# Chunked attention and a multiplicative FFN on one core: first loads reordered, first four units turned on TensorE, DMA turns moved later

## Chip, cores, metric

One core of a Trainium2 chip. Times are device microseconds (us) of one execution. A quoted time is the median of its runs; before and after were run at least three times each. Ratios are the mean time of one kernel's fast runs over that of the other's fast runs of the same rounds, so not quite the ratio of the medians. An interval in brackets is the 95% interval of that ratio. Where nothing else is said, the runs quoted are fast ones (no run more than 1.5% above the fastest of its kernel). The engines: PE is TensorE (PEld its weight loads), DVE VectorE, ACT ScalarE, POOL GpSimd, and SP SyncE, which here only issues DMAs. A DMA *lands* when the last of its completion signals comes in the trace.

## The reference, cut to what matters

```python
# q, k, v: [B=8, H=8, S=576, D=64] float32; chunks of 64 tokens, softmax within the chunk
scores = (q_chunk @ k_chunk.T) / sqrt(D);  attn = softmax(scores);  o = attn @ v_chunk
x = o.transpose(0, 2, 1, 3).reshape(4608, 512)          # 4608 tokens, 512 channels
out = ((x @ w1) * (x @ w2)) @ w3 @ w_out                # d_ff = 1024
```

The kernel computes in bf16 and multiplies `w3 @ w_out` once, in the prologue (`w3o`).

## The kernel before, where it matters

A *unit* is 128 tokens, two chunks: 36 units, 4.5 per sequence. An FFN tile takes 512 tokens, four units. To *turn* a tile means to transpose it in 128x128 blocks. q and k arrive token by token and must be turned before the scores; the attention result `xn` is turned into `xt` before the FFN. All turns are DMA transposes issued by SP, in program order, from SBUF to SBUF. All loads, which also cast float32 to bf16 (the page counts 38.8 MB read from HBM and 19.4 MB moved by GpSimd's queue), are issued by GpSimd. Matmuls, turns and loads each keep their program order.

```python
def load(dst, src): return inorder(nc.gpsimd.dma_start(dst, src))
def turn(dst, src): return inorder(nc.sync.dma_start_transpose(dst, src))

def turn_qk(b, i0, i1): ...        # cut: up to three turns, of q, k and the last half unit, of sequence b

def do_PV(u):
    ...                            # cut: products into PSUM, reciprocal, multiplication into xn
    turn(xt[:, :, u * UT:(u + 1) * UT], xn[:].rearrange("p n t d -> p (n t d)"))

# prologue: loads with turns between them; sequence 1 is turned before any x
load_w(wo, ...); load_w3(0); load_qk(0, 0); turn_qk(0, 0, 1); load_w3(1); load_qk(0, 1); turn_qk(0, 1, 2)
load_v(0)                          # 8 loads, one for each head
...                                # cut: rest of sequence 0, w3, w1, w2
load_batch(1); load_v(1); turn_qk(1, 0, NP + 1); load_batch(2); load_v(2)

def S_step(u):                     # scores; at a change of sequence all of the next one is turned
    do_S(u)
    b = (2 * u + 2) // NCH
    if b != (2 * u) // NCH and b + 1 < B:
        turn_qk(b + 1, 0, NP + 1)
        if b + 2 < B: load_batch(b + 2)

for u in range(UPT + 1): ...       # cut: w3 transposes, w3o and attention of units 0 to 3
# FFN tile t (16 groups of matmuls), with attention of the units of tile t+1 between its groups,
# and the output matmuls of tile t-1
```

The softmax here doesn't subtract the row's maximum and nothing guards it: scores larger than these inputs give would overflow.

## Time and profile before

| | before |
|---|---|
| median time (runs) | 325.7 us (322.4 to 326.9) |
| span of the profiled run | 323.9 us |
| first FFN matmul | 82.7 us |
| TensorE (PE) busy, whole span | 243 us, 75% |
| PE waits of over 0.5 us after the first FFN matmul | 25.5 us |

The page of the kernel before has the span in 40 slices of 8.1 us. A digit is the busy share in tenths; `PEclk` is the granted clock.

```profile
PE   0248067007899302999988996999999999999995
PEclk9987667655999855999997998999999999999999
DMA  7999999999999999999999999796593141231113
```

PE has two holes of over 19 us, in slices 8 and 9 and in slices 14 to 16. The DMA engines are busy for about 25 slices, 200 us. Stretches say the same in numbers (the columns are named in the first line):

```profile
core 0: us, PE busy (x) PEld busy (x) DVE busy (x) ACT busy (x) POOL busy (x), PEclk, DMA share, GB/s
83.00:200.00 117.00, 91.51 (x916) 42.38 (x914) 36.75 (x66) 35.42 (x62) 61.83 (x78) 0.90 1.74 157
200.00:324.00 124.00, 120.13 (x973) 55.27 (x971) 41.00 (x70) 44.44 (x78) 5.86 (x8) 0.98 0.46 92
```

So there is a *loading phase*, with the DMA moving 157 GB/s, in which PE is busy 78% of the time, and after 200 us a phase in which PE is busy 97%. PE's timeline shows the ends of the holes. In the brackets are the idle time before and what ended it:

```profile
74.67 0.44 PE L59 MATMUL xp<-vbuf_80,e 64*64 64x65 bf16 x16 [19.75 <-DVE xn L174]
...
82.67 7.07 PE L59 MATMUL a_ps<-xt,w_74 128*128 128x512 bf16 x32 [1.16 <-DMA xt<-xn]
...
127.36 1.89 PE L59 MATMUL a_ps<-xt,w_74 128*128 128x512 bf16 x4 [19.48 <-DMA xt<-xn]
```

SP's timeline has the cause. Its columns are the start and the time that SP itself was held; a line of several turns (x4) runs from the first start to the last end, waits between them included:

```profile
57.17 3.71 SPq L69 DMA_TRANSPOSE qT<-q_sb  x1
61.06 4.51 SPq L69 DMA_TRANSPOSE kT<-k_sb  x1
65.68 1.20 SPq L69 DMA_TRANSPOSE qkT<-qk_sb  x1
66.98 10.41 SPq L69 DMA_TRANSPOSE xt<-xn  x4
...
104.98 6.14 SPq L69 DMA_TRANSPOSE qT<-q_sb  x1
111.29 7.33 SPq L69 DMA_TRANSPOSE kT<-k_sb  x1
118.78 1.21 SPq L69 DMA_TRANSPOSE qkT<-qk_sb  x1
120.09 23.73 SPq L69 DMA_TRANSPOSE xt<-xn  x5
```

x of units 0 to 3 is turned from 67 us on, behind the turns of sequence 1, which wait for their data; x of unit 7 is turned at 120 us, behind those of sequence 3. The first hole ends with products (`xp`) and not with the FFN, because the multiplication into `xn` waited for one of its two buffers, which an x turn sets free: by the view of the tile xn, it waited 23.3 us for x turns.

### The profile page before, as it was taken

Reading aid. Unit: us, or ns where it says so; the run is one execution under the profiler, and the core shown is the slowest. Engines: PE = TensorE matmul, PEld = TensorE weight load, DVE = VectorE, ACT = ScalarE, POOL = GpSimd, SP = SyncE. Lnnn points to the kernel's source line nnn. Section 1 sums busy time; section 2 is a strip of 40 time slices with the busy share of each in tenths; the row PEclk is TensorE's granted clock in tenths of the full one; section 3 lists DMA queues with packets and bytes.
Section 4 is the critical chain, followed back from the end, with each engine's and each line's share of the span. In section 5 each row is a group of like instructions: output and inputs, shape, how many; then the busy total and the mean of one; then the engine's idle time right before and its main releaser. Section 6 shows DMA issues by size and latency. Waiting matters only on the chain.

```text
span 323.9 us, 5311 instructions
## 1 busy us (share of the span) xinstructions
PE 243.1 (75%) x2144; PEld 113.4 (35%) x2144; DVE 87.1 (27%) x155; ACT 88.1 (27%) x153; POOL 123.1 (38%) x163
## 2 busy tenths in 40 slices
PE   0248067007899302999988996999999999999995
PEld 0214033003344101444433442444444444444442
DVE  0001111002064100454331332334334343341310
ACT  1011012000523200343341432343343333423232
POOL 8486425967719725902940880070000000000000
PEclk9987667655999855999997998999999999999999
DMA  7999999999999999999999999796593141231113
GB/s 96 175 148 178 177 195 163 180 172 139 171 162 142 180 155 156 144 88 180 158 150 212 131 154 209 122 115 116 120 157 69 49 97 53 80 68 50 47 67 130
DMA packets 179816, 43.35 MB, mean 134 GB/s; under 512 B 171088, under 2 KB 174160, under 8 KB 179792
## 3 DMA queue, kind: packets, MB, share of 16 engines
q0 software_dynamic: 117200, 19.41, 86.6%
q1 hardware_dynamic: 57408, 14.16, 29.4%
q10 hardware_dynamic: 5184, 9.44, 9.1%
q8 instruction: 17, 0.28, 0.4%
q14 instruction: 7, 0.06, 0.1%
HBM read 38.80 MB, written 9.44 MB: 149 GB/s over the span
## 4 chain that ended last, share of the span: by engine, by line
PE 61%; DMA 27%; POOL 5%; issue 3%; SPq 2%; DVE 1%; ACT 0%; POOLq 0%; DVEq 0%
PE a_ps L59 20%; PE b_ps L59 20%; PE o_ps L59 17%; DMA xt<-xn 9%; DMA w_75<-in_moe_w_dram 6%; DMA k_sb<-in_k_dram 3%; DMA w_76<-in_moe_w_dram 3%; PE sp L59 3%; DMA q_sb<-in_q_dram 3%; DMA vbuf_80<-in_v_dram 2%; SPq L69 2%; DMA vbuf_81<-in_v_dram 2%; PE xp L59 2%; POOL vbuf_81 L65 1%; POOL vbuf_80 L65 1%
## 5 line engine op out<-in xcount | busy, mean ns | idle before, releaser
L59 PE MATMUL a_ps<-xt,w_74 128*128 128x512 bf16 x288 | 75.9, 391 | 26.1 <-DMA xt<-xn 23.2
L198 DVE TENSOR_TENSOR ab<-a_sb,b_ps 128x512 bf16<-128x512 f32 x72 | 49.5, 688 | 113.3 <-PE b_ps L59 113.3
L59 PE MATMUL b_ps<-xt,w_75 128*128 128x512 bf16 x288 | 75.8, 390 | 0.0
L59 PE MATMUL o_ps<-w3o,ab 128*128 128x512 bf16 x288 | 67.3, 379 | 0.0
L191 ACT COPY a_sb<-a_ps 128x512 f32<-128x512 f32 x72 | 42.1, 585 | 83.0 <-PE a_ps L59 76.6
L59 PEld LDWEIGHTS <-w_74 128*128 128x128 bf16 x288 | 26.5, 100 | 57.1 <-DMA xt<-xn 19.6
L59 PEld LDWEIGHTS <-w_75 128*128 128x128 bf16 x288 | 28.7, 100 | 35.5 <-issue 3.4
L59 PEld LDWEIGHTS <-ab 128*128 128x128 bf16 x288 | 27.9, 98 | 33.4
L210 ACT COPY o_sb<-o_ps 128x512 f32<-128x512 f32 x36 | 21.1, 586 | 66.6 <-PE o_ps L59 66.6
L65 POOL DMA_DIRECT2D k_sb<-in_k_dram x32 | 30.2, 943 | 7.9 <-DMA w_75<-in_moe_w_dram 2.5
L65 POOL DMA_DIRECT2D q_sb<-in_q_dram x32 | 30.3, 947 | 6.6 <-DMA w_75<-in_moe_w_dram 2.5
L174 DVE TENSOR_TENSOR xn<-xp,rc 128x512 bf16<-128x512 f32 x36 | 24.9, 692 | 24.6 <-DMA xt<-xn 23.3
L65 POOL DMA_DIRECT2D vbuf_81<-in_v_dram x24 | 17.5, 750 | 30.8 <-PE xp L59 19.0
L155 ACT ACTIVATE e<-sp 128x512 bf16<-128x512 f32 x36 | 21.6, 601 | 22.3 <-PE sp L59 21.5
L65 POOL DMA_DIRECT2D vbuf_80<-in_v_dram x24 | 17.6, 760 | 24.6 <-PE xp L59 20.2
L59 PE MATMUL sp<-qT,kT 64*64 64x64 bf16 x512 | 14.9, 197 | 12.6 <-DMA kT<-k_sb 12.6
L59 PE MATMUL wp<-wo,w3T 128*128 128x512 bf16 x64 | 22.5, 520 | 0.0
L229 ACT CAST w3o<-wp 128x512 bf16<-128x512 f32 x8 | 4.7, 585 | 60.1 <-PE wp L59 60.1
L62 PE MATMUL w3tp<-ident,w_76 128*128 128x128 bf16 x64 | 7.1, 278 | 18.0 <-DMA w_76<-in_moe_w_dram 18.0
L59 PE MATMUL xp<-vbuf_80,e 64*64 64x65 bf16 x216 | 5.7, 202 | 19.7 <-DVE xn L174 19.7
L172 DVE RECIPROCAL rc<-xp 128x8 f32<-128x8 f32 x36 | 7.4, 207 | 47.7 <-PE xp L59 47.6
L59 PEld LDWEIGHTS <-kT 64*64 64x64 bf16 x512 | 11.0, 110 | 25.6 <-DMA kT<-k_sb 13.3
(25 smaller groups left out, 76.1 us busy)
## 6 DMA issues: line engine op xcount, KB each, us to landing
out_dram<-o_sb ACTq DMA_DIRECT2D x36, 256.0 KB, 2.2
q_sb<-in_q_dram POOLq DMA_DIRECT2D x32, 128.0 KB, 8.0
k_sb<-in_k_dram POOLq DMA_DIRECT2D x32, 128.0 KB, 8.0
w_76<-in_moe_w_dram POOLq DMA_DIRECT2D x8, 256.0 KB, 8.9
vbuf_80<-in_v_dram POOLq DMA_DIRECT2D x24, 72.0 KB, 4.3
vbuf_81<-in_v_dram POOLq DMA_DIRECT2D x24, 72.0 KB, 5.0
vbuf_82<-in_v_dram POOLq DMA_DIRECT2D x16, 72.0 KB, 5.7
wo<-in_moe_w_out_dram POOLq DMA_DIRECT2D x1, 1024.0 KB, 9.5
```

What stands on the lines that cost most here:

```text
L59: return inorder(nc.tensor.matmul(*a, **kw))
L62: return inorder(nc.tensor.transpose(*a, **kw))
L65: return inorder(nc.gpsimd.dma_start(dst, src))
L69: return inorder(nc.sync.dma_start_transpose(dst, src))
L155: nc.scalar.activation(e[:], sp[:], Exp, scale=scale, bias=0.0)
L172: nc.vector.reciprocal(rc[:], xv[:, :, :, D:D + 1])
L174: nc.vector.tensor_mul(xn[:].rearrange("p n t d -> p t n d"), xv[:, :, :, 0:D], rc.to_broadcast([P, 2, NHP, D]))
L191: nc.scalar.copy(a_t[j][:], a_ps[:])
L198: nc.vector.tensor_mul(ab_t[t][:, j, :], a_t.pop(j)[:], b_ps[:])
L210: nc.scalar.copy(o_sb[:], o_ps[:])
L229: nc.scalar.copy(w3o[:, ko, :], wp[:])
```

## The change

Intent: let the FFN start earlier. The first four units no longer need the DMA for turns (PE transposes them, between the groups of `w3 @ w_out`), loads come in an order that serves this and in larger pieces, and turns of later sequences no longer stand ahead of x. The second FFN tile is halved, so that its first half needs two units only. Besides, q/k get three buffers instead of two, `xn` three as well, the heads lie in another order in the buffers, and the scores use four 64x64 quadrants of the array (`64*64` in the trace) in turn instead of two.

```diff
 def load_v(b):                                   # two loads instead of eight
-    for h in range(H): load(vbuf[...one head...], v[b, h]...)
+    for t in range(2): load(vbuf[...four heads...], v[b, t * NHP:(t + 1) * NHP]...)
-    qk_t[b] = (io.tile(q, bufs=2), io.tile(k, bufs=2), io.tile(qk, bufs=2))
+    qk_t[b] = io.tile([P, G, DM], bf, tag="qk", bufs=3)        # nine groups: q, k, q, k, ..., last
+def pe_turn_qk(b, g):
+    tp = ps.tile([P, NHP, P], bf, tag="m", bufs=4)
+    for n in range(NHP): tr(tp[:, n, :], qk_t[b][:, g, n * P:(n + 1) * P], ident[:])
+    nc.vector.tensor_copy(qkT_tile(b)[:, g], tp[:])
+def pe_turn_x(u): ...                            # the same from xn to xt
-load_w3(0); load_qk(0,0); turn_qk(0,0,1); load_w3(1); ...; load_batch(1); load_v(1); turn_qk(1, ...)
+load_w3(0,1); load_w3(1,2); load_qk(0,0); load_qk(0,1); load_w3(2,3); load_v(0); ...   # no turns here
-for u in range(UPT + 1): do_S(u); do_w3T(u + 2); do_w3o(u + 1); PV_step(u - 1)
+do_w3T(0); do_w3T(1); do_w3o(0); pe_turn_unit(0); pe_turn_unit(1); do_w3o(1); ...; pe_turn_x(3); do_w3o(7)
+tiles = [(0, 512), (512, 256), (768, 256), (1024, 512), ...]
+pieces = ((0, 4), (4, 8), (8, 9))                # turns of the next sequence, one piece each at
 def S_step(u):                                   # chunks 2, 4 and 6 of this one
-    turn_qk(b + 1, 0, NP + 1)
+    if b > 1 and c in (2, 4, 6): turn_qk(b + 1, *pieces[c // 2 - 1])
+    if b == 1 and c == 7: ...                    # all pieces of sequence 2
```

(Scores, buffers and placing of the steps are shortened.)

More of the change, by code (lines that the diff above doesn't have):

```diff
@@ L82 @@
         nc.vector.memset(vbuf[i][:, :, :, D:D + 1], 1.0)
+    NP = S // UT
+    G = 2 * NP + 1
     qk_t, qkT_t = {}, {}
-    NP = S // UT
     def rows(src, b, t0, n):
@@ L94, in load_qk @@
         if b not in qk_t:
-            qk_t[b] = (io.tile([P, NP, DM], bf, tag="q", name="q_sb"),
-                       io.tile([P, NP, DM], bf, tag="k", name="k_sb"),
-                       io.tile([P, DM], bf, tag="qk", name="qk_sb"))
+            qk_t[b] = io.tile([P, G, DM], bf, tag="qk", bufs=3, name="qk")
         if i < NP:
-            for t, src in zip(qk_t[b], (q, k)):
-                load(t[:, i, :].rearrange("p (h d) -> p h d", d=D), rows(src, b, i * UT, UT))
+            for t, src in enumerate((q, k)):
+                load(qk_t[b][:, 2 * i + t, :].rearrange("p (h d) -> p h d", d=D),
+                     rows(src, b, i * UT, UT))
@@ L101, in load_qk @@
         else:
             for p0, src in ((0, q), (CH, k)):
-                load(qk_t[b][2][p0:p0 + CH, :].rearrange("p (h d) -> p h d", d=D),
+                load(qk_t[b][p0:p0 + CH, 2 * NP, :].rearrange("p (h d) -> p h d", d=D),
                      rows(src, b, NP * UT, CH))
-    def turn_qk(b, i0, i1):
-        if b not in qkT_t:
-            qkT_t[b] = (io.tile([P, NP * NHP, P], bf, tag="qT", name="qT"),
-                        io.tile([P, NP * NHP, P], bf, tag="kT", name="kT"),
-                        io.tile([P, NHP, P], bf, tag="qkT", name="qkT"))
-        if i0 < NP:
-            i = min(i1, NP)
-            for t in range(2):
-                turn(qkT_t[b][t][:, i0 * NHP:i * NHP, :],
-                     qk_t[b][t][:, i0:i, :].rearrange("p c m -> p (c m)"))
-        if i1 > NP:
-            turn(qkT_t[b][2][:], qk_t[b][2][:])
@@ L119, in qT, with load_batch @@
-    def qT(b, c, hp):
-        if c // 2 < NP:
-            return qkT_t[b][0][:, c // 2 * NHP + hp, c % 2 * CH:(c % 2 + 1) * CH]
-        return qkT_t[b][2][:, hp, 0:CH]
-    def kT(b, c, hp):
-        if c // 2 < NP:
-            return qkT_t[b][1][:, c // 2 * NHP + hp, c % 2 * CH:(c % 2 + 1) * CH]
-        return qkT_t[b][2][:, hp, CH:P]
+    def load_batch(b):
+        for i in range(NP + 1):
+            load_qk(b, i)
     def load_v(b):
-        for h in range(H):
-            n, hh = divmod(h, 2)
-            load(vbuf[b % NV][hh * CH:(hh + 1) * CH, n, :, 0:D],
-                 v[b, h].rearrange("(c p) d -> p c d", p=CH))
+        for t in range(2):
+            load(vbuf[b % NV][t * CH:(t + 1) * CH, :, :, 0:D].rearrange("p n c d -> p (n c) d"),
+                 v[b, t * NHP:(t + 1) * NHP].rearrange("n (c p) d -> p (n c) d", p=CH))
@@ L135, in load_w, with qkT_tile, turn_qk @@
     def load_w(dst, ap, n0, n1):
         load(dst[:, :, n0:n1], ap.rearrange("(ko p) n -> p ko n", p=P)[:, :, n0:n1])
+    def qkT_tile(b):
+        if b not in qkT_t:
+            qkT_t[b] = io.tile([P, G, NHP, P], bf, tag="qkT", name="qkT")
+        return qkT_t[b]
+    def turn_qk(b, g0, g1):
+        turn(qkT_tile(b)[:, g0:g1].rearrange("p g n t -> p (g n) t"),
+             qk_t[b][:, g0:g1, :].rearrange("p g m -> p (g m)"))
+    def pe_turn_qk(b, g):
+        tp = ps.tile([P, NHP, P], bf, tag="m", bufs=4, name="qktp")
+        for n in range(NHP):
+            tr(tp[:, n, :], qk_t[b][:, g, n * P:(n + 1) * P], ident[:])
+        nc.vector.tensor_copy(qkT_tile(b)[:, g], tp[:])
@@ L139, in chunk_at, with at @@
+    def at(b, c, n, isk):
+        i, o = divmod(c, 2)
+        if i < NP:
+            return qkT_t[b][:, 2 * i + isk, n, o * CH:(o + 1) * CH]
+        return qkT_t[b][:, 2 * NP, n, isk * CH:(isk + 1) * CH]
     def chunk_at(u, ci):
         return divmod(2 * u + ci, NCH)
-    e_t = {}
+    NM = NHP // 2
+    e_t, xn_t = {}, {}
     def do_S(u):
-        sp = ps.tile([P, NHP, 2, CH], f32, tag="s", name="sp")
+        sp = ps.tile([P, 2, 512], f32, tag="s", name="sp")
+        sv = sp[:, :, 0:NHP * CH].rearrange("p r (m c q) -> p r m c q", m=NM, c=2)
@@ L146, in do_S @@
         for ci in range(2):
             b, c = chunk_at(u, ci)
-            for hp in range(NHP):
-                for hh in range(2):
-                    h = slice(hh * CH, (hh + 1) * CH)
-                    mm(sp[h, hp, ci, :],
-                       lhsT=kT(b, c, hp)[h], rhs=qT(b, c, hp)[h],
-                       start=True, stop=True)
-        e = asb.tile([P, NHP, 2, CH], bf, tag="e", name="e")
-        nc.scalar.activation(e[:], sp[:], Exp, scale=scale, bias=0.0)
+            for m in range(NM):
+                for t in range(2):
+                    for r in range(2):
+                        h = slice(r * CH, (r + 1) * CH)
+                        mm(sv[t * CH:(t + 1) * CH, r, m, ci, :],
+                           lhsT=at(b, c, 2 * t + m, 1)[h], rhs=at(b, c, 2 * t + m, 0)[h],
+                           start=True, stop=True)
@@ L156, in do_S @@
+        e = asb.tile([P, 2, NM, 2, CH], bf, tag="e", name="e")
+        nc.scalar.activation(e[:].rearrange("p r m c q -> p r (m c q)"), sp[:, :, 0:NHP * CH],
+                             Exp, scale=scale, bias=0.0)
         e_t[u] = e
@@ L161, in do_PV @@
         W = D + 1
-        for hp in range(NHP):
-            for ci in range(2):
-                b, c = chunk_at(u, ci)
-                for hh in range(2):
-                    h = slice(hh * CH, (hh + 1) * CH)
-                    mm(xp[ci * CH:(ci + 1) * CH, hh, hp * W:(hp + 1) * W],
-                       lhsT=e[h, hp, ci, :], rhs=vbuf[b % NV][h, hp, c, 0:W],
-                       start=True, stop=True)
+        for m in range(NM):
+            for r in range(2):
+                for ci in range(2):
+                    b, c = chunk_at(u, ci)
+                    for t in range(2):
+                        h = slice(t * CH, (t + 1) * CH)
+                        n = 2 * m + r
+                        mm(xp[ci * CH:(ci + 1) * CH, t, n * W:(n + 1) * W],
+                           lhsT=e[h, r, m, ci, :], rhs=vbuf[b % NV][h, n, c, 0:W],
+                           start=True, stop=True)
         xv = xp[:, :, 0:NHP * W].rearrange("p t (n w) -> p t n w", w=W)
@@ L172, in do_PV, with turn_x, pe_turn_x @@
         nc.vector.reciprocal(rc[:], xv[:, :, :, D:D + 1])
-        xn = asb.tile([P, NHP, 2, D], bf, tag="xn", name="xn")
-        nc.vector.tensor_mul(xn[:].rearrange("p n t d -> p t n d"), xv[:, :, :, 0:D],
-                             rc.to_broadcast([P, 2, NHP, D]))
-        turn(xt[:, :, u * UT:(u + 1) * UT], xn[:].rearrange("p n t d -> p (n t d)"))
+        xn = asb.tile([P, 2, NHP, D], bf, tag="xn", bufs=3, name="xn")
+        nc.vector.tensor_mul(xn[:], xv[:, :, :, 0:D], rc.to_broadcast([P, 2, NHP, D]))
+        xn_t[u] = xn[:].rearrange("p t n d -> p (t n d)")
+    def turn_x(u):
+        turn(xt[:, :, u * UT:(u + 1) * UT], xn_t.pop(u))
+    def pe_turn_x(u):
+        xn = xn_t.pop(u)
+        tp = ps.tile([P, NHP, P], bf, tag="m", bufs=4, name="xtp")
+        for n in range(NHP):
+            tr(tp[:, n, :], xn[:, n * P:(n + 1) * P], ident[:])
+        nc.vector.tensor_copy(xt[:, :, u * UT:(u + 1) * UT], tp[:])
+    tiles = [(0, TT), (TT, TT // 2), (TT + TT // 2, TT // 2)]
+    tiles += [(t0, TT) for t0 in range(2 * TT, NT, TT)]
     ab_t, a_t = {}, {}
     def mm_ab(w, dst, t, j):
-        xs = xt[:, :, t * TT:(t + 1) * TT]
+        t0, n = tiles[t]
         for ki in range(KO):
-            mm(dst[:], lhsT=w[:, ki, j * P:(j + 1) * P], rhs=xs[:, ki, :],
+            mm(dst[:, 0:n], lhsT=w[:, ki, j * P:(j + 1) * P], rhs=xt[:, ki, t0:t0 + n],
                start=(ki == 0), stop=(ki == KO - 1))
     def do_a(t, j, tag="a_sb", bufs=2):
+        n = tiles[t][1]
         a_ps = ps.tile([P, TT], f32, tag="m", bufs=4, name="a_ps")
@@ L190, in do_a @@
         a_t[j] = msb.tile([P, TT], f32, tag=tag, bufs=bufs, name="a_sb")
-        nc.scalar.copy(a_t[j][:], a_ps[:])
+        nc.scalar.copy(a_t[j][:, 0:n], a_ps[:, 0:n])
     def do_b(t, j):
+        n = tiles[t][1]
         if t not in ab_t:
@@ L197, in do_b @@
         mm_ab(w2, b_ps, t, j)
-        nc.vector.tensor_mul(ab_t[t][:, j, :], a_t.pop(j)[:], b_ps[:])
+        nc.vector.tensor_mul(ab_t[t][:, j, 0:n], a_t.pop(j)[:, 0:n], b_ps[:, 0:n])
     def do_ab(t, j):
@@ L210, in do_o @@
         nc.scalar.copy(o_sb[:], o_ps[:])
-        r0 = t * TT + n * P
+        r0 = tiles[t][0] + n * P
         inorder(nc.scalar.dma_start(out[r0:r0 + P, :], o_sb[:]))
@@ L219, in do_w3T @@
             tr(tp[:, ki, :], w3[:, ko, ki * P:(ki + 1) * P], ident[:])
-        w3T_t[ko] = msb.tile([P, FO, P], bf, tag="w3T", name="w3T")
+        w3T_t[ko] = msb.tile([P, FO, P], bf, tag="w3T", bufs=3, name="w3T")
         nc.vector.tensor_copy(w3T_t[ko][:], tp[:])
@@ L232, with load_w3 @@
     w3v = moe_w3.rearrange("(ko p) n -> p ko n", p=P)
-    def load_w3(ko):
-        load(w3[:, ko, :], w3v[:, ko, :])
-    def load_batch(b):
-        for i in range(NP + 1):
-            load_qk(b, i)
+    def load_w3(k0, k1):
+        load(w3[:, k0:k1, :], w3v[:, k0:k1, :])
     load_w(wo, moe_w_out, 0, DM)
@@ L245 @@
         fill=1.0, base=0, pattern=[[-1, P]], channel_multiplier=1))
-    load_w3(0)
+    load_w3(0, 1)
+    load_w3(1, 2)
     load_qk(0, 0)
-    turn_qk(0, 0, 1)
-    load_w3(1)
     load_qk(0, 1)
-    turn_qk(0, 1, 2)
+    load_w3(2, 3)
     load_v(0)
-    load_w3(2)
+    load_w3(3, 4)
     load_qk(0, 2)
-    turn_qk(0, 2, 3)
-    load_w3(3)
     load_qk(0, 3)
-    load_qk(0, 4)
-    turn_qk(0, 3, 5)
-    for ko in range(4, FO):
-        load_w3(ko)
+    load_w3(4, 6)
+    load_w3(6, 8)
     HF = DF // 2
@@ L265 @@
             load_w(w, ap, n0, n0 + HF)
-    load_batch(1)
+    load_qk(0, 4)
+    load_qk(1, 0)
+    load_qk(1, 1)
     load_v(1)
-    turn_qk(1, 0, NP + 1)
+    for i in range(2, NP + 1):
+        load_qk(1, i)
     load_batch(2)
     load_v(2)
+    pieces = ((0, 4), (4, 8), (8, 9))
     def S_step(u):
         do_S(u)
-        b = (2 * u + 2) // NCH
-        if b != (2 * u) // NCH and b + 1 < B:
-            turn_qk(b + 1, 0, NP + 1)
-            if b + 2 < B:
-                load_batch(b + 2)
+        for ci in range(2):
+            b, c = chunk_at(u, ci)
+            if b == 0:
+                continue
+            if c == 0 and b + 2 < B:
+                load_batch(b + 2)
+            if b + 1 < B:
+                if b > 1 and c in (2, 4, 6):
+                    turn_qk(b + 1, *pieces[c // 2 - 1])
+                if b == 1 and c == 7:
+                    for p in pieces:
+                        turn_qk(2, *p)
     def PV_step(u):
         do_PV(u)
+        turn_x(u)
         b = (2 * u + 2) // NCH
@@ L285, in PV_step, with pe_turn_unit @@
             load_v(b + 2)
+    def pe_turn_unit(i):
+        pe_turn_qk(0, 2 * i)
+        pe_turn_qk(0, 2 * i + 1)
     do_w3T(0)
@@ L289, with place @@
     do_w3o(0)
-    for u in range(UPT + 1):
-        if u < UPT:
-            do_S(u)
-        if u + 2 < FO:
-            do_w3T(u + 2)
-        do_w3o(u + 1)
-        if u > 0:
-            PV_step(u - 1)
+    pe_turn_unit(0)
+    pe_turn_unit(1)
+    do_w3o(1)
+    do_w3T(2)
+    do_S(0)
+    do_w3o(2)
+    do_S(1)
+    do_PV(0)
+    do_w3T(3)
+    do_w3o(3)
+    do_PV(1)
+    pe_turn_unit(2)
+    pe_turn_unit(3)
+    pe_turn_x(0)
+    do_w3T(4)
+    do_S(2)
+    do_w3T(5)
+    do_w3o(4)
+    pe_turn_x(1)
+    do_S(3)
+    do_PV(2)
+    do_w3T(6)
+    do_w3o(5)
+    do_PV(3)
+    pe_turn_x(2)
     do_w3T(7)
     do_w3o(6)
+    pe_turn_x(3)
     do_w3o(7)
-    fill, slots = [], {}
+    fill, units = [], {}
+    def place(d, *what):
+        units.setdefault(len(fill) + d, []).extend(what)
     for j in range(FO):
@@ L307 @@
         fill.append(lambda j=j: do_b(0, j))
-    slots[14] = (UPT, None)
-    slots[15] = (UPT + 1, UPT)
-    slots[16] = (UPT + 2, UPT + 1)
-    slots[17] = (UPT + 3, UPT + 2)
-    slots[18] = (UPT + 4, UPT + 3)
+    place(-2, lambda: (turn_qk(0, 8, 9), turn_qk(1, 0, 2), turn_qk(1, 2, 4)))
+    place(0, lambda: S_step(4), lambda: turn_qk(1, 4, 6))
+    place(1, lambda: S_step(5))
+    place(2, lambda: PV_step(4))
+    place(3, lambda: PV_step(5), lambda: turn_qk(1, 6, 8), lambda: turn_qk(1, 8, 9))
     for n in range(UPT):
         fill.append(lambda n=n: do_o(0, n))
-    for t in range(1, NTT):
-        for n in range(UPT):
-            if t + 1 < NTT:
-                u = (t + 1) * UPT + n
-                slots[len(fill)] = (u + 1, u)
+    place(0, lambda: S_step(6))
+    place(2, lambda: S_step(7))
+    place(3, lambda: PV_step(6))
+    place(5, lambda: PV_step(7))
+    for j in range(FO):
+        fill.append(lambda j=j: do_ab(1, j))
+    place(0, lambda: S_step(8))
+    us = list(range(8, NU))
+    for t in range(2, len(tiles)):
+        no = tiles[t - 1][1] // P if t > 1 else 0
+        for n in range(4):
+            if us:
+                u = us.pop(0)
+                if u + 1 < NU:
+                    place(0, lambda u=u: S_step(u + 1))
+                place(0, lambda u=u: PV_step(u))
             fill.append(lambda t=t, j=2 * n: do_ab(t, j))
             fill.append(lambda t=t, j=2 * n + 1: do_ab(t, j))
-            if t > 1:
+            if n < no:
                 fill.append(lambda t=t, n=n: do_o(t - 1, n))
     for n in range(UPT):
-        fill.append(lambda n=n: do_o(NTT - 1, n))
+        fill.append(lambda n=n: do_o(len(tiles) - 1, n))
     for i, f in enumerate(fill):
-        if i in slots:
-            us, up = slots[i]
-            if us < NU:
-                S_step(us)
-            if up is not None:
-                PV_step(up)
+        for g in units.get(i, ()):
+            g()
         f()
```

## The prediction

> **What bounds the kernel now.** From about 130 us TensorE (PE) is nearly full: the stretches 140-160 and 200-280 show it busy throughout; one 512-token FFN tile with attention takes 23.1 us. Before that it starves: the timeline has the first FFN matmul at 82.7 us, after only some 30 us of PE work. The large holes are 55-74.7 and 107.9-127.4 us. The chain of waits explains the first: loads until w2 lands (51.05), then q/k and v of sequence 1, then SP turns q/k of sequence 1, and only then x of sequence 0. In SP's timeline x of unit 0, whose xn is done at 33 us, is turned at 67, behind three turns of sequence 1. The second hole is alike: x of unit 7 queues behind q/k turns of sequence 3 (105-119).
>
> **What the change does.**
> 1. Sequence 0's first four units need no DMA turn: 32 PE transposes of q/k and 16 of x, 4-5 us of PE (a w3 group of 8 takes 0.62-1.04), 12 more copies of about 0.7 us on DVE, 27% busy. Gone: x waiting for sequence 1, and 1.5 MB of turns.
> 2. Loads: v in 2 instead of 8, w3 partly in pairs. Each load waits for the one eight before it, so larger ones keep more in flight. Loads alone land at about 157 GB/s of bf16 (128 KB each 0.84 us). The 6.9 MB up to w2 are through at about 44 us (51 before, shared with turns). Estimate.
> 3. Second FFN tile halved: its first half needs only units 4 and 5.
> 4. Turns go in pieces between the x turns.
> 5. Scores use four 64x64 quadrants instead of two; S+PV cost 0.6 us per unit (steps of 5.79 against 5.18); I expect 0.1 less each, 3 us in all.
>
> **Sum.** PE starts at 12 us (wo and first w3, unchanged) with 33 us of dense prologue work, so out of the half-speed state that follows idling (w3o groups of 8 take 3.2 us after a hole, 1.89 without[...]). First FFN matmul at about 49 us, 34 earlier. Tile 0 with outputs ends at 71. New stalls follow, because each next tile's x is computed just before its use, and a turn takes 0.9 us on DVE plus 6-7 to land under load: 6 us before the first half tile, 7 around S of unit 9 (turns of sequence 2 sit behind x of unit 7), 5 before tile 3, 3 later. Tile 3 starts at about 112; one tile of 19 us, five of 22.8, a last of 20.7, 10 of tail: 283 plus 2 outside the profiled span.
>
> DMA limits this: a 512-token tile costs it about 10 us of loads, 8 of turns (198 GB/s alone at 200-205 us), 3 of output, 21 of PE's 23. So waits on xt may grow.
>
> **Predicted: 286 us, range 276 to 301.** Faster by over 2%: 0.97; within 2%: 0.02; slower: 0.01.
>
> **Signs.** First a_ps matmul at 46-53 us; the holes at 55-75 and 108-127 gone; several 3-8 us waits of PE for xt or qkT between 70 and 115; steady tiles at 22.5-23 us; SP's first turn after 44 us.
>
> **What would make it wrong.** DMA saturating after 70 us, so that late turns stall PE in every tile (300 or more); hand-offs holding the prologue (FFN at 55+); shorter landings, which erase the stalls (275).

Four things that the prediction says of the hardware, as before shows them:

- Four w3o groups of 8 soon after holes of 1.7 to 9.0 us took 3.15 to 3.45 us; two that followed such work without a hole took 1.89. From 60 to 75 us, in a hole, the granted clock was 0.50. It was 0.54 to 0.60 in three of the slow groups, but 1.00 in the fourth (at 15.86 us), whose slowness it therefore does not show.
- The ninth load was issued at 11.07 us, after a wait of 2.86 us that the landing of the first (wo) ended. That larger loads keep more in flight was an estimate.
- Loads alone moved 154 GB/s from 54 to 57 us.
- The packets of the output queue took 9.1% of the 323.9 us span, 3.3 us for each of nine tiles.

## More of the kernel before

The experiments ran later, on three chips, where the median of before was 323.7 to 326.5 us; where a comparison with after hangs on a few us, the ratios are the safer measure.

The FFN of tile t+1 needs x of all its units. The products of its last unit run only two pairs of FFN groups (3.5 us) and one output group (1.7 us) before it starts.

How long a turn of x takes from its issue to its landing is in the view of the tile xt:

```profile
DMA to landing us min/median/max: 2.4/4.4/7.5
```

## The result

| | before | after |
|---|---|---|
| median time (runs) | 325.7 us | 313.3 us (312.1 to 313.7) |
| ratio | | 0.963 [0.957, 0.970] |
| span of the profiled run | 323.9 us | 311.3 us |
| first FFN matmul | 82.7 us | 40.0 us |
| PE waits of over 0.5 us after it | 25.5 us | 52.4 us |
| rest of the span (span less the two) | 215.7 us | 218.9 us |

The FFN starts 42.6 us sooner, and the kernel ends 12.6 us sooner by the profile. The last two rows say where the other 30 us went: 26.9 us into new waits of PE, 3.2 us into the rest. The slices of the page after (7.8 us each):

```profile
PE   0497999909319604993999229989999999999995
PEclk9999999967958955999699859997999999999999
DMA  6999999999999999999999997992275322311013
```

The prologue is now dense, and behind it are five large holes. The DMA row hardly changed. The stretches of after:

```profile
40.00:190.00 150.00, 99.70 (x997) 50.43 (x996) 39.12 (x76) 38.49 (x73) 67.97 (x78) 0.82 1.88 157
190.00:311.00 121.00, 115.40 (x958) 52.14 (x956) 39.90 (x69) 43.28 (x76) 2.30 (x2) 0.98 0.44 94
```

This is the whole result in two lines. The loading phase still runs at 157 GB/s, and it ends near 190 us, not much earlier than before: by the trace the last q/k load lands at 190.6 us (199.7 in before). PE entered it 43 us sooner, but was busy for 99.7 us of it (66%), where before it was busy for 91.5 us. PE's timeline shows the waits:

```profile
40.03 7.07 PE L59 MATMUL a_ps<-xt,w_74 128*128 128x512 bf16 x32
...
64.91 0.33 PE L59 MATMUL sp<-qkT 64*64 64x64 bf16 x8 [2.39 <-DMA qkT<-qk]
70.48 1.01 PE L59 MATMUL a_ps<-xt,w_74 128*128 128x256 bf16 x4 [5.25 <-DMA xt<-xn]
...
92.40 0.43 PE L59 MATMUL sp<-qkT 64*64 64x64 bf16 x16 [11.54 <-DMA qkT<-qk]
...
109.52 0.32 PE L59 MATMUL sp<-qkT 64*64 64x64 bf16 x8 [3.25 <-DMA qkT<-qk]
...
121.04 1.89 PE L59 MATMUL a_ps<-xt,w_74 128*128 128x512 bf16 x4 [10.98 <-DMA xt<-xn]
122.73 1.91 PE L59 MATMUL b_ps<-xt,w_75 128*128 128x512 bf16 x4
...
148.56 1.86 PE L59 MATMUL a_ps<-xt,w_74 128*128 128x512 bf16 x4 [5.89 <-issue]
...
184.53 1.86 PE L59 MATMUL a_ps<-xt,w_74 128*128 128x512 bf16 x4 [11.00 <-issue]
```

"issue" in the last two means that the view found no releaser close by; the x turns that these tiles need landed at 148.47 and 184.44 us, 0.09 us ahead of each, so they too are waits for x. After a wait the first groups ran at half speed: from 121.04 us on, two groups of four matmuls start 1.69 us apart, against 0.86 to 0.87 in a steady stretch of a tile (129 to 132 us). The granted clock was 0.50 from 121.0 to 124.4 us and 1.00 from 156 to 172 us; after the waits that ended at 70.5, 92.4 and 148.6 us it was 0.50 too (for the next 2.5 to 3.5 us), after the one at 184.5 us 0.60.

The wait at 184 is the one to study. Its x is that of unit 19, whose products are done by 168 us. SP's timeline of after:

```profile
166.22 1.64 SPq L69 DMA_TRANSPOSE xt<-xn  x1
168.06 7.56 SPq L69 DMA_TRANSPOSE qkT<-qk  x1
175.73 1.26 SPq L69 DMA_TRANSPOSE xt<-xn  x1
```

SP was held for 7.56 us by issuing a 512 KB turn of q/k, then issued the turn of x at 175.73, and that landed at 184.44, 8.7 us later: 17 us from products to use, with 5 us of matmuls to cover them. The turn of q/k itself had landed only at 182.29, 2.15 us before x, so part of these 8.7 us may be time behind it on the same queue. It can't be all of it: the x turns issued at 130.24 and 157.62, when every earlier turn had landed, still took 7.1 and 8.0 us. The view of the tile xt, after:

```profile
DMA to landing us min/median/max: 2.4/6.9/9.8
```

The minimum is as before; the median went from 4.4 to 6.9 us. Two theories suggested themselves. **Volume**: in the loading phase the DMA must move its bytes at 157 GB/s, and PE can't run ahead of them. **Landing**: the bytes suffice, but a few turns that PE needs at once take 7 to 17 us because other traffic is in their way.

### The profile page after: what moved, and what is told of

The parts are those of the page before. It is cut to its first block, busy times and chain, and to the rows that moved or that the text cites. A ratio compares the mean times of both kernels' runs of the same rounds, so it can differ in the third digit from the quotient of the medians.

```text
span 311.3 us, 5443 instructions
## 1 busy us (share of the span) xinstructions
PE 240.8 (77%) x2256; PEld 117.6 (38%) x2256; DVE 92.2 (30%) x175; ACT 89.4 (29%) x161; POOL 93.8 (30%) x113
## 4 chain that ended last, share of the span: by engine, by line
PE 68%; DMA 22%; issue 4%; DVE 3%; POOL 1%; SPq 1%; ACT 0%; DVEq 0%; POOLq 0%
PE a_ps L59 21%; PE b_ps L59 19%; PE o_ps L59 18%; DMA xt<-xn 16%; PE wp L59 5%; DMA qkT<-qk 4%; DMA w_76<-in_moe_w_dram 3%; PE sp L59 2%; PE xp L59 2%; DVE xn L181 1%; PE w3tp L62 1%; DVE w3T L241 1%; DVE qkT L130 1%; SPq L69 1%; DVE ab L218 0%
## 5 line engine op out<-in xcount | busy, mean ns | idle before, releaser
L59 PE MATMUL a_ps<-xt,w_74 128*128 128x512 bf16 (+1 forms) x320 | 80.9, 383 | 35.2 <-DMA xt<-xn 18.3
L218 DVE TENSOR_TENSOR ab<-a_sb,b_ps 128x512 bf16<-128x512 f32 (+1 forms) x80 | 50.7, 634 | 126.9 <-PE b_ps L59 126.6
L59 PE MATMUL b_ps<-xt,w_75 128*128 128x512 bf16 (+1 forms) x320 | 78.8, 375 | 0.0
L210 ACT COPY a_sb<-a_ps 128x512 f32<-128x512 f32 (+1 forms) x80 | 43.4, 543 | 90.9 <-PE a_ps L59 89.6
L59 PEld LDWEIGHTS <-w_74 128*128 128x128 bf16 x320 | 30.4, 103 | 65.6 <-issue 25.7
L65 POOL DMA_DIRECT2D qk<-in_k_dram x40 | 34.1, 853 | 42.6 <-DMA qk<-in_k_dram 17.9
L59 PEld LDWEIGHTS <-w_75 128*128 128x128 bf16 x320 | 32.7, 102 | 34.5 <-issue 5.1
L65 POOL DMA_DIRECT2D qk<-in_q_dram x40 | 34.1, 852 | 28.0 <-DMA qk<-in_q_dram 11.5
L159 ACT ACTIVATE e<-sp 128x512 bf16<-128x512 f32 x36 | 21.6, 601 | 27.0 <-PE sp L59 26.9
L59 PE MATMUL sp<-qkT 64*64 64x64 bf16 x576 | 12.2, 202 | 17.2 <-DMA qkT<-qk 17.2
L59 PEld LDWEIGHTS <-qkT 64*64 64x64 bf16 x576 | 7.9, 110 | 30.7 <-DMA qkT<-qk 17.5
L65 POOL DMA_DIRECT2D vbuf_81<-in_v_dram x6 | 6.9, 1149 | 19.0 <-PE xp L59 14.5
## 6 DMA issues: line engine op xcount, KB each, us to landing
qk<-in_q_dram POOLq DMA_DIRECT2D x32, 128.0 KB, 12.6
qk<-in_k_dram POOLq DMA_DIRECT2D x32, 128.0 KB, 12.6
```

The lines of the kernel that those rows point to most:

```text
L59: return inorder(nc.tensor.matmul(*a, **kw))
L159: nc.scalar.activation(e[:].rearrange("p r m c q -> p r (m c q)"), sp[:, :, 0:NHP * CH], Exp, scale=scale, bias=0.0)
L210: nc.scalar.copy(a_t[j][:, 0:n], a_ps[:, 0:n])
L218: nc.vector.tensor_mul(ab_t[t][:, j, 0:n], a_t.pop(j)[:, 0:n], b_ps[:, 0:n])
```

## The experiments

All are edits of the kernel after unless said otherwise. Each kernel gave four runs, beside seven or eight of before on the same chip. "Waits" are PE's idle times of over 0.5 us after its first FFN matmul, in the profiled run.

### Bytes or landings: e2, e4, e9

**e2_x_on_pe.** All x are turned on PE, one pair of FFN groups after their products.

```diff
 def PV_step(u):
-    do_PV(u); turn_x(u)
+    do_PV(u)
+    place(1, lambda u=u: pe_turn_x(u))     # one step later; likewise for units 4 to 7
```

> Every x is turned on PE (4 transposes and one DVE copy per unit) instead of by DMA, for all units and not only the first four. Both A and B expect it to gain: 3.7 MB of turns leave the DMA (23 us at 156 GB/s) and the 35 us of waits for xt go, for about 28 x 0.35 = 10 us more PE work. A: 285-292. B: 288-296, with waits for qkT growing. If instead PE or DVE hand-offs cost more than thought: over 300.

Measured: 279.7 us, ratio to before 0.864 [0.859, 0.869]. That is 34 us below after (32 by the ratios), and below both ranges expected, for a few moved lines; 32 turns left the DMA, not the 28 that the expectation counted. Waits 15.6 us. The slices and the stretch of the loading phase:

```profile
PE   0297899993987907999999999999999999999993
DMA  6999999999999999999999999999971111111223
```

```profile
40.00:190.00 150.00, 133.86 (x1421) 69.34 (x1420) 60.45 (x122) 51.62 (x97) 70.51 (x80) 0.94 1.91 160
```

The DMA is as busy as ever (160 GB/s until 190 us), yet PE is busy 89% of the phase. A busy DMA was not in itself the limit.

**e4_qk_part_on_pe.** The control: nearly as many bytes of turns taken from the DMA, but turns of q/k.

```diff
-    if b > 1 and c in (2, 4, 6): turn_qk(b + 1, *pieces[c // 2 - 1])
+    if b > 1 and c == 2:                    # and at c == 7 of sequence 1; groups 0-3 of sequence 1 too
+        for g in range(4): pe_turn_qk(b + 1, g)
+    if b > 1 and c in (4, 6): turn_qk(b + 1, *pieces[c // 2 - 1])
```

> Control for e2_x_on_pe: the same number of turns (28 of 128 KB, 3.7 MB) leaves the DMA for PE, but they are turns of q/k (the first four groups of sequences 1 to 7); all x after the first four units stays on the DMA. If e2 gained its 34 us by relieving the DMA of bytes (volume), this gains about the same: 278-288. If e2 gained because nothing waits for the landing of an x turn any more (latency), the waits for xt stay, shortened, and only the 17 us of waits for qkT go: 295-303.

Measured: 307.2 us, ratio 0.943 [0.939, 0.947]. The waits for qkT went, those for x stayed, as the view of waits has it for e4 (who waited for what: us in total, times, longest):

```profile
PE a_ps L59 <- DMA xt<-xn: 37.6, 6, 12.2
```

The trace has 38.1 MB moved in e4 and 37.6 in e2, of 41.8 in after. So 3.7 MB off the DMA gained 6 us here, and 4.2 MB gained 34 us in e2. Part of this contrast is PE's own: in the profiled runs e4's waits fell by 14.8 us, but the rest of its span grew by 7.0, with 28 more groups of transposes on PE; in e2, with 32 more, waits fell by 36.8 and the rest grew by 2.3. Volume is refuted as the chief cause; what counts is that PE does not wait for an x turn to land.

**e9_no_late_loads.** Sequences 4 to 7 are not loaded, everything else stays. Its output is wrong, which doesn't matter for the time.

```diff
 def load_qk(b, i):
+    if b > 3: qk_t[b] = qk_t[3]; return
 def load_v(b):
-    for t in range(2): load(...)
+    for t in range(2 if b < 4 else 0): load(...)
```

> Wrong result on purpose: q, k and v of sequences 4 to 7 are not loaded (their turns and products use sequence 3's data, and v buffers as they stand); every turn, wait order and matmul stays. After about 110 us the DMA then carries turns and outputs only. If the x turns land late because loads share the DMA engines: an x turn then lands in 2.4-5 us and the waits at 142 and 173 (17 us) and most of that at 110 (11 us) go: 288-298. If SP's order alone makes them late (an x turn issued behind a 512 KB turn of q/k): waits stay at 5-8 us each: 302-310.

Measured: 282.9 us, ratio 0.870 [0.864, 0.877]. This is below the 288 to 298 expected; the waits at 142 and 173 us are gone, as expected, and the last wait ends at 116 us. SP's timeline of e9:

```profile
145.24 2.03 SPq L69 DMA_TRANSPOSE qkT<-qk  x1
149.26 1.19 SPq L69 DMA_TRANSPOSE xt<-xn  x1
150.50 1.83 SPq L69 DMA_TRANSPOSE qkT<-qk  x1
154.92 2.28 SPq L69 DMA_TRANSPOSE xt<-xn  x1
```

From 120 to 190 us a 512 KB turn now holds SP for 1.3 to 2.9 us, against 5.5 to 7.6 in after. The view of DMA issues in the stretch 120 to 190 us (count, median us to landing), first of after, then of e9:

```profile
xt<-xn SPq DMA_TRANSPOSE x8, 8.1
```

```profile
xt<-xn SPq DMA_TRANSPOSE x13, 2.4
```

With the order on SP unchanged and only the loads gone, an x turn lands in 2.4 us instead of 8.1. So loads that share the DMA slow the turns, and they lengthen SP's hold as well. (With the loads, the q/k turns' waits for their data went too; the 7.56 us hold at 168 us in after was not such a wait: the semaphore that this issue waits for did not change in that time.) This pair of runs shows what a queue of loads costs a short turn beside it: 5.7 us.

### Can order or pacing cure it: e1, e1b, e8, e3, u1, u2, u4

**e1_paced** and **e1b_paced_earlier.** Loads are held back until PE has reached a point 14 or 18 chunks ahead of their use: a one-element copy on ACT from the scores' result, and one on GpSimd that waits for it ahead of the loads.

```diff
+LEAD = 14                                        # e1b: 18
+def paced_loads(u):                              # called in S_step after do_S(u)
+    todo = [(b, i) for ci in range(2) for b in range(3, B) for i in range(NP + 1)
+            if NCH * b - LEAD + 2 * i == 2 * u + ci]
+    if todo:
+        inorder(nc.scalar.copy(gate[:, u, 0:1], e_t[u][0:1, 0, 0, 0, 0:1]))
+        inorder(nc.gpsimd.tensor_copy(gate[:, u, 1:2], gate[:, u, 0:1]))
+        for b, i in todo: load_qk(b, i)
-    if c == 0 and b + 2 < B: load_batch(b + 2)
```

> Same kernel as after, but each q/k load of sequences 3 to 7 is held back until the tensor engine has done the scores 14 chunks ahead of its use. Theory A (contention): the turns that PE waits for are slow (7-14 us to land against 2.4 us on an idle DMA) because they share the DMA engines with loads that are needed only 30-60 us later. Then the waits for xt at 142.7 (5.9 us) and 173.5 (11.0 us) all but go, that at 110 (11.0 us) shrinks, and the time falls from 313 to 292-300. Theory B (volume): from 40 to 190 us the DMA just has to move its bytes at about 156 GB/s, in whatever order; then holding loads back gains nothing: 311-316, and waits only move.

> e1_paced held loads back too far: its turns of the last piece waited for their data on SP, with x turns queued behind them, and the DMA stood idle at 130-135 and 160-165. Here the loads start 18 chunks ahead, not 14. If contention with loads that are not yet needed slows x turns: 300-308, waits for xt at 140-190 shorter than the 17 us of after. If not: 311-318.

Measured: e1 326.2 us, ratio 1.008 [1.003, 1.013], a miss. Some turns of q/k then waited on SP for their late data, with x turns behind them (one until 150.66 us; the x behind it landed at 157.21 and ended a wait of 9.6 us), and at other times the DMA had nothing to do: from 130 to 135 us it moved nothing at all. e1b: ratio 0.965 [0.959, 0.971] from its fast runs (312.8 and 315.4 us; the other two, 319.0 and 319.7, count as slow), no gain over after. By its expectation that counts against contention, but the pacing did not take the loads out of the way: x turns issued from 120 to 190 us still took 7.9 us to land (median; 8.1 in after). In e1 they took 5.9, and the late data cost more than that gained. Pacing in these two forms cures nothing; a better form is not excluded.

**e8_x_first.** The q/k turn of a slot is issued after its x turn.

```diff
 def PV_step(u):
     do_PV(u); turn_x(u)
+    ...                                          # the pieces of chunk_at(u + 1), moved here from S_step
```

> From unit 7 on, the q/k turns of a slot are issued after its x turn, not before it. In after, x of unit 19 is issued 8.2 us after its products, as SP is held for 7.6 us by the issue of a 512 KB turn of q/k. If that head-of-line hold counts: the wait at 173 falls from 11.0 to 4-6 us, that at 110 by 2-5 us: 303-309. If landing under load is what counts: 311-316.

Measured: 319.2 us, ratio 0.983 [0.975, 0.992]: 6 us slower than after, and outside both ranges expected: a miss. SP's timeline of e8 suggests why: x now stands behind the q/k turn of the slot before (the x below landed at 158.56 us and ended a wait of 11.9 us).

```profile
143.33 7.88 SPq L69 DMA_TRANSPOSE qkT<-qk  x1
151.31 1.50 SPq L69 DMA_TRANSPOSE xt<-xn  x1
```

**e3_two_units_ahead.** Attention runs two units further ahead of the FFN from the third tile on.

```diff
+if us and t in (2, 3) and n == 1:
+    u = us.pop(0); place(0, lambda u=u: S_step(u + 1)); place(0, lambda u=u: PV_step(u))
```

> Attention runs two units further ahead of the FFN from the third tile on, so that a landing time of 10 us is covered by 11 us of matmuls. If the loss is only the landing time of the last x of each tile (theory C, latency): the waits at 142.7, 173.5 and 208.6 (19 us) go, 294-297. B (volume): 311-315, PE then waits for qkT instead. A (contention) lies between, 296-306, as the loads still slow the turns.

Measured: 301.2 us, ratio 0.931 [0.928, 0.935]. More matmuls between products and use recover 12 us of the 34, but 41 us of waits remain, of which 19 are for qkT. A result between the theories, as expected of contention.

**u1_full_tile, u2_whole_turns, u4_two_qk_buffers.** Each undoes one part of the change.

```diff
# u1                                              # units 4 to 7 before the second tile
-tiles = [(0, TT), (TT, TT // 2), (TT + TT // 2, TT // 2)] + ...
+tiles = [(t0, TT) for t0 in range(0, NT, TT)]
# u2
-    if b > 1 and c in (2, 4, 6): ...             # pieces
+    if c == 0 and b + 1 < B:
+        for p in pieces: turn_qk(b + 1, *p)
# u4                                              # loads of sequences 2 and 3 moved behind the turns they wait for
-    qk_t[b] = io.tile([P, G, DM], bf, tag="qk", bufs=3, name="qk")
+    qk_t[b] = io.tile([P, G, DM], bf, tag="qk", bufs=2, name="qk")
```

> One part undone: the second FFN tile has 512 tokens again, so it waits for x of units 4 to 7. If the halving earns what it was made for, PE stalls about 15 us before that tile in place of 8+11 us around two half tiles; all later waits alike. Latency view: 311-318. Volume view: no change, 312-315.

> One part undone: q/k of the next sequence turned all at once when the sequence changes, as in the kernel before, not in later pieces. If the later pieces are what created the 11.5 us wait of the scores of unit 9 (turn of sequence 2 issued at 80 us, behind x of unit 7), this wait goes, but x of the following units queues behind 1.2 MB of turns; if the order on SP matters little (B): 311-316. If the pieces were worth something: 317-325.

> One part undone: two q/k buffers as in the kernel before, so a load waits for the turns of the sequence two before it. If the third buffer's eagerness is what keeps the DMA loaded while x turns wait: 300-309. If pacing by buffers is no better than the pacing of e1b: 311-318. If loads then come late: over 320.

Measured: u1 313.7 us (0.962 [0.958, 0.966]), u2 309.7 us (0.956 [0.951, 0.960]), u4 308.4 us (0.948 [0.941, 0.956]; one run of 313.7 counted as slow). After has 0.963. The halved tile is worth nothing measurable: PE's waits come to 53.7 us in u1 and 52.4 in after. By the ratios the later turns cost 2 to 3 us, but the intervals of u2 and after overlap, so this is not shown. The third buffer seems to cost about 5 us; u4 also moved two loads, so it is not a clean undoing. In u2 the scores of unit 6 wait 22 us for the turns of sequence 1, which there stand behind those of sequence 2, and it is still no slower: other waits shrank.

### What the early start is worth: u3, e10

**u3_first_on_dma.** q/k and x of the first four units go back to DMA turns, in the new order.

```diff
 def pe_turn_unit(i):
-    pe_turn_qk(0, 2 * i); pe_turn_qk(0, 2 * i + 1)
+    turn_qk(0, 2 * i, 2 * i + 2)
-pe_turn_x(0) ... pe_turn_x(3)
+turn_x(0) ... turn_x(3)
```

> One part undone: q/k and x of the first four units turned by DMA as in the kernel before, in the new order, with nothing ahead of them on SP. The first FFN matmul comes at 52-60 us and not at 40. If the head start was given back because the DMA could not follow anyway, the end moves by less than half of that: 315-321. If waits later are independent of the start, it moves by all of it: 326-333.

Measured: 333.4 us, ratio 1.025 [1.019, 1.030]: slower than before, though whether by 2% is unclear. FFN starts at 60.9 us, 20.9 later than in after, and the end moves by 20 us. This mixes two things, the later start and 1.5 MB more turns on the DMA, which e10 separates.

**e10_late_start.** PE does 96 dummy matmuls before the first FFN tile; the DMA's work is untouched.

```diff
     do_w3o(7)
+    for i in range(12):
+        dp = ps.tile([P, DM], f32, tag="m", bufs=4, name="dp")
+        for ki in range(FO):
+            mm(dp[:], lhsT=wo[:, ki, 0:P], rhs=wo[:, ki, :], start=(ki == 0), stop=(ki == FO - 1))
```

> The kernel after with 96 dummy matmuls (20.7 us) on PE before the first FFN tile; DMA and all else untouched. If the head start of the change is worth nothing while the loads run (each tile that falls into the loading phase pays a late x turn, a later start has fewer such tiles): waits shrink by 15-20 us, the end moves by less than 6: 312-319. If waits do not depend on when PE starts: 331-335.

```profile
61.06 4.26 PE L59 MATMUL a_ps<-xt,w 128*128 128x512 bf16 x19
```

Measured: 326.8 us, ratio 1.008 [1.000, 1.016]. The start moved by 21.0 us, the span by 10.8 (the medians by 13.5, by the ratios 14), and the waits fell from 52.4 to 42.8 us. The profiled run was the fastest of e10's four, so the medians are the better measure of what is kept. So neither expectation: of these 21 us of head start a third to a half is given back to waits, the rest is kept. Of the 20 us that u3 lost, 11 to 14 are then the later start, and what remains goes with its additional DMA turns.

### Without the x turn, what remains: e5, e7, e12, e11

**e5_no_dma_turns.** e2, and all q/k turned on PE too.

```diff
-    ...turn_qk(b + 1, piece)...
+    gs = range(c, c + 1) if b > 1 else range(9) if c == 7 else ()
+    for g in gs: pe_turn_qk(b + 1, g)            # likewise sequence 1, in tile 0
```

> No DMA turn at all: x and q/k of every sequence are turned on PE. The DMA is left with 19.4 MB of loads and the outputs, done near 150 us; nothing waits for a landing but first loads. PE gets 63 more groups of 4 transposes than e2 has (minus its first 8), at about 0.3 us each 16 us. Latency view: all DMA waits of e2 (12 us) go, more PE work by 16: 280-288. If PE and DVE hand-offs in line cost more: 290-300.

Measured: 280.8 us, ratio 0.865 [0.859, 0.870], as e2. Waits after the start of the FFN are 1.3 us; 64 more groups of transposes than in e2 ran on PE, and the span less start and waits grew from 221.2 to 238.1 us, which ate what the waits gave.

**e7_x_on_pe_early_turns.** e2, with q/k turns issued earlier and a third qkT buffer.

```diff
-    if b > 1 and c in (2, 4, 6): turn_qk(b + 1, *pieces[c // 2 - 1])
+    if c in (0, 2, 4): turn_qk(b + 1, *pieces[c // 2])
-    qkT_t[b] = io.tile([P, G, NHP, P], bf, tag="qkT", name="qkT")
+    qkT_t[b] = io.tile([P, G, NHP, P], bf, tag="qkT", bufs=3, name="qkT")
-VW = 96
+VW = 80
```

> Candidate for best: e2_x_on_pe, with the q/k turns issued as soon as data and a third qkT buffer allow (v rows 160 bytes apart instead of 192, to make room). e2 still waits 8.4 us at 97 and 2.3 at 63 for qkT. If these are landings of turns issued late: both shrink, 268-274. If the DMA can't deliver them sooner (volume): 277-281.

Measured: 292.8 us, ratio 0.901 [0.893, 0.908]: 13 us slower than e2, a miss. The wait at 97 us stayed (9.3 us), and two new ones came, of 3.3 and 6.9 us, for ACT, which had stood still while it waited to issue an output. By its timeline the landing of a q/k turn ended that stop at 125.5 us. How the output came to wait for that turn was not tested.

**e12_before_x_on_pe.** The kernel *before*, with only its x turned on PE.

```diff
 def do_PV(u):
-    turn(xt[:, :, u * UT:(u + 1) * UT], xn...)
+    xn_t[u] = xn...                              # xn with 3 buffers; pe_turn_x(u) one step later
```

> The kernel before, with every x turned on PE and nothing else of the change. If the x turn on the DMA is the chief loss in both kernels: the holes at 55-75 and 108-127 shrink to what q/k turns and loads cost, some 30 us less, 10 us more PE work: 300-308. The rest of the change (start at 40 instead of about 60 us) would then be worth the other 20-28 us between this and e2's 280.

Measured: 292.7 us (288.4 to 295.5), ratio 0.894 [0.882, 0.906]. Two of its four runs, the profiled one too, count as slow, so the ratio rests on two runs and the size is rough; even the slowest lies 18 us below after, and all are below the 300 to 308 expected. FFN starts at 58.1 us. The one cure, put on the old kernel (with the third `xn` buffer that after has too), is worth more than the whole change.

**e11_x_on_pe_tuned.** e2, with the q/k groups that it still waits for on PE, and four output buffers.

```diff
-    place(0, lambda: S_step(4), lambda: turn_qk(1, 4, 6))
+    place(0, lambda: S_step(4)); place(1, lambda: (pe_turn_qk(1, 4), pe_turn_qk(1, 5)))
+    if b == 2 and c == 2:
+        for g in range(4): pe_turn_qk(3, g)
-    o_sb = msb.tile([P, DM], f32, tag="o_sb", name="o_sb")
+    o_sb = msb.tile([P, DM], f32, tag="o_sb", bufs=4, name="o_sb")
```

> Candidate for best: e2_x_on_pe, with the q/k groups whose turns it still waits for (fifth and sixth of sequence 1, first four of sequence 3) turned on PE, and four output buffers in place of two, since ACT waited for outputs to land. e2 has 2.3 + 8.4 us of qkT waits and 2.7 us of ACT; PE gets 2 us more: 266-273. If new waits take their place: 276-282.

Measured: 272.7 us (272.4 to 273.2), ratio 0.840 [0.834, 0.845]: the fastest of all, 53 us below before and 41 below after. Its slices:

```profile
PE   0297899998687899999999999999999999999993
```

## Why the prediction was wrong

It said 286 us, 276 to 301; 313.3 us came. Its sum, by terms of the profiled span:

| term | predicted | measured in after |
|---|---|---|
| first FFN matmul | 49 us | 40.0 us |
| PE waits after it (6 + 7 + 5 + 3) | 21 us | 52.4 us |
| rest: PE work and tail | 213 us | 218.9 us |
| span | 283 us | 311.3 us |

- **The start** was right in kind and even too cautious: 34 us predicted, 42.6 us measured. The prologue took 28.4 us from PE's first matmul, not 33, and w2 landed at 41.4 us, not 44.
- **The step that failed** is "6 us before the first half tile, 7 around S of unit 9 (...), 5 before tile 3, 3 later". The first came as 2.4 + 5.3 us, the second as 11.5, the third as 3.3 + 11.0, and "3 later" as 5.9 + 11.0 + 2.1 = 19 us. The cause was named, each tile's x computed just before its use, but it was taken to end with tile 3. It went on as long as the loads did: the waits for x before tiles 4, 5 and 6 ended at 148.6, 184.5 and 210.7 us, and the last load landed at 208 us. In before, the same lateness cost only 5 us after 130 us, and that was carried over without asking why. The head start is a part of the why: by the profiled runs e10 shows that starting 21 us sooner turns about 10 us of it into waits. More tiles then fall into the loading phase, which fits (eight waits against six) but was not shown apart.
- **"A turn takes 0.9 us on DVE plus 6-7 to land under load"** left out a term. 8.1 us is the median landing in after from 120 to 190 us, longer than the 5.8 us of before in the same stretch, and ahead of it SP was held for 5.5 to 7.6 us by issuing a 512 KB q/k turn; e9 shows both as effects of the loads (2.4 us, and 2 us).
- **"DMA limits this ... 21 of PE's 23"** set the wrong kind of limit beside roughly right numbers (its 3 us of output is too little: outputs alone moved at most 262 GB/s over 1 us of before, so by our estimate the 1.05 MB of a tile takes 4 us; the 198 GB/s of turns is what before moved from 200 to 205 us, with a short pause in it). With 3.7 MB less, e4 gained 6 us; with 4.2 MB less, and no x to wait for, e2 gained 34. Here the DMA's occupancy bounded PE far less than the time that single transfers took on it. The first of the things said to make it wrong, late turns stalling PE tile by tile, is what came, but through landing times and not through lack of bandwidth.
- **"Turns go in pieces between the x turns"** and the halved second tile were listed among what the change does. u2 shows no gain from the pieces, and u1 none from the halved tile.
- **The scores in four quadrants** fit what was said: the step from one unit's products to the next in the quiet phase fell from 5.78 to 5.66 us, 0.1 us per unit; no run undoes them alone. The restarts at half speed after waits (granted clock 0.50 to 0.60 after five of them) were not in the sum; they can explain why the rest did not fall with it (from 121.04 us on, after a wait, two FFN pairs took 5.83 us; the next two took 3.46 us). This part is read from the trace and was not tested alone.

What stays open: why a 512 KB turn holds SP for longer beside loads; the share of loads, of q/k turns ahead on the queue and of SP's hold in each wait (e8 moved the hold and gained nothing; no run took all q/k turns off the DMA and left x on it); and what a finer pacing of the loads would bring. The change may also have made its own landings slower: from 120 to 190 us q/k loads of 128 KB took a median of 6.2 us to land in before and 13 to 14 in after, at 152 and 155 GB/s. The third q/k buffer seems one reason (u4: 6.9 us, but x turns still 7.2); the loads of v, four times as large now, are another candidate, and no run undoes them.

## What to carry to other kernels

A DMA that the compute engine needs at once should be costed at its landing time beside the traffic of that phase (here 128 KB of x: 8.1 us beside loads, 2.4 us without them), and at the time its queue is held by the transfer ahead of it (here up to 7.6 us), not at its bytes. Before making a stage start earlier, ask which phase its later work will then fall into, and what that phase does to its shortest waits. Where a small transpose stands between two matmuls, try it on TensorE: here four of them (0.39 us as a row, in after) and a copy, in place of a DMA turn, lengthened the step of a unit in the quiet phase by 0.22 us (5.66 in after, 5.88 in e2), some 7 us over 32 units, and took 36.8 us of waits away (52.4 to 15.6); the time fell by 34 us, more than the whole change had brought.
